# Steps 2 to 15 of a fused attention and two-layer kernel, written as one list of operations

## The chip, the cores and the metric

One core of a Trainium2 chip. The metric is the device time of one execution in microseconds. PE is TensorE, DVE is VectorE, ACT is ScalarE, POOL is GpSimd, SP is SyncE, whose queue issues the DMAs.

## The reference

Chunked attention (batch 4, 8 heads, 768 positions of 64; chunks of 32 queries see 16 positions to the left, 8 to the right and 8 memory slots), then two dense layers over 3072 tokens, 512 wide with 2048 inside:

```
for each chunk c:
    k_full = concat(mem_k, k[c*32-16 : c*32+40]);  v_full likewise
    a = softmax(q_c @ k_full.T / 8)
    out[c] = a @ v_full
x = out as 3072 x 512
x = relu(x @ moe_w_in)**2 @ moe_w_out
h = x @ moe2_w_in
return (h * tanh(softplus(h))) @ moe2_w_out
```

## The kernel before

The tokens are cut into three blocks `sb` of 1024 (four pairs `p` of 128-token tiles each, so p runs from 0 to 11), and the inner width into eight parts `j` of 256. A step is one part of one block of one layer: steps 0 to 23 are the first layer (block `s // 8`, part `s % 8`), steps 24 to 47 the second. In a step of the first layer the first weight matrix is multiplied by Strassen's scheme in the Winograd form: seven products (`product`, L587), each of six matmuls of 128x128 weights with 512 columns. Their order by name is P1, P6, P5, P2, P7, P4, P3; they accumulate in PSUM banks 0 to 2. DVE and ACT take partial sums out of the banks (`u`, L941, L948, L967) and form the four quarters of the result (L969, L975, L980), ACT applies ReLU and square (L606, L607) and rounds to a high part `g` (L600), and POOL subtracts it to give the low part (L601). The second weight matrix then takes eight units of six matmuls (`unit`, L700) in banks 3 to 5, each added by DVE to the output `y` (L714) or copied by ACT for the first part (L712). Units of step s-1 are interleaved with the products of step s. A step so has 90 matmuls of 512 columns.

Beside these run, on all engines: the attention of the next block of tokens (scores L396, maximum L414, exponentials L433, division L448 on POOL, transposes L461, their copies L482, values L506, copies L526 and sums L535 to L539 on POOL); the decoding of weights, which arrive as 64-bit numbers in halves of 512 KB (`rebias` L158 on ACT, `decode` L165 to L169 on DVE, sums L181 to L185, rounding L207 on ACT and subtraction L213 on DVE for the first layer, L225 and L232 for the second, whose parts are stored to DRAM as `w_d`); and the reading back and splitting of the blocks `x` of the next tokens (`load_x`, `split_x`, L308 on ACT and L310 on DVE). From step 8 on the first layer's weights are streamed from DRAM again, in pieces of 256 KB (`stream_w`, L259). Raw weights are loaded three halves ahead; a load is put aside by `later` and issued by the next `flush` (L141).

Steps 0 and 1 with the attention before them are a written list of single operations (the string at L1057). From step 2 (`BEGUN`) on `step` gives the order: after each product and each unit it calls `rest`, the next of 15 points of a step, which issues the weight streams and what the plans have put there with `at` (`plan_attention` at a period of 22 points, `plan_w`, `plan_sums`, and the loads and splits of x):

```
def rest():
    flush()
    i = point[0]
    if NQ <= s + 1 < STEPS and i % 2 == 0 and i < POINTS - 1:
        stream_w(s + 1, 0, i // 2)
    ...
    for w in beside.pop((s, point[0]), []):
        w()
    point[0] += 1
```

Each engine runs its instructions in the order in which they are issued here.

Of the kernel before, what the change touches and what calls it, by code (L numbers as in the profile page):

```python
# [26 lines left out]
NB = 512  # L27
# [29 lines left out]
BEGUN = 2  # L57
POINTS = 15
# [4 lines left out]
def tile_chunk_attention_moe_moe2(  # L63
# [569 lines left out]
    def block(i, s):  # L633
        ps, start, stop = {
            "1": (0, True, False), "2": (0, False, True), "6": (1, True, False), "5": (2, True, False),
            "7": (1, False, False), "4": (1, False, True), "3": (2, False, True),
        }[i]
        product(int(s), {"1": P1, "2": P2, "3": P3, "4": P4, "5": P5, "6": P6, "7": P7}[i], bank(ps), start, stop)

    def keep(i, s):  # L640
        u = u_t[i, s] = ring("u", 3, [128, NB], FP32, "u")
# [11 lines left out]
    def gated(part, s, key):  # L653
# [8 lines left out]
        elif part == "c":  # L662
            g = g_t[int(s), of[key]] = pool.tile([128, 2, NB], FP32R, tag=f"g{(4 * int(s) + i) % 7}", name="g")
            nc.scalar.copy(out=g[:, 0], in_=h_t[s, key])
        else:
            g = g_t[int(s), of[key]]
            nc.gpsimd.tensor_tensor(out=g[:, 1], in0=h_t[s, key], in1=g[:, 0].bitcast(FP32), op=ALU.subtract)

    def first_unit(i):
        w = w2_t[0].rearrange("p c (b f) -> p c b f", b=4)  # L670
        t, d = i // 4, i % 4
        order = [(f, a, 0) for f in range(2) for a in range(2)] + [(f, 0, 1) for f in range(2)]
        for n, (f, a, c) in enumerate(order):
            nc.tensor.matmul(
                out=bank(3 + i % 3),
                lhsT=w[:, a, (2 + f, f)[d // 2], d % 2 * 128:d % 2 * 128 + 128],
                rhs=g_t[0, (f, t)][:, c, :],
# [122 lines left out]
    def plan_attention(s, i, p, begun=-1):  # L800

        for n, work in {
            0: lambda: scores(p),
            1: lambda: softmax(p, 0),
            2: lambda: softmax(p, 1),
            3: lambda: (exps(p, 0), load_k(p + 1) if (p + 1) % PSB else None),
            4: lambda: exps(p, 1),
            6: lambda: normalize(p),
            8: lambda: load_v(p) if p > PSB else None,
            13: lambda: transpose_p(p),  # L810
            14: lambda: (copy_pt(p), load_q(p + 1) if (p + 1) % PSB else None),
            17: lambda: values(p),
            18: lambda: copy_x(p),
            19: lambda: sums_x(p, nc.gpsimd),
            22: lambda: store_x(p) if p != 2 * PSB - 1 else None,
        }.items():
            if n > begun:
                at(s, i + n, work)

    def plan_sums(sb):  # L820
# [32 lines left out]
        at(s, 5, lambda: later(d[:, B11], blocks()[0]))  # L853
        at(s, 9, lambda: later(d[:, B21], blocks()[1]))
        at(s, 13, first)
        at(s + 1, 0, second)
        at(s + 1, 1, fourth)
        at(s + 1, 3, third)
# [137 lines left out]
    with tc.manual_schedule():  # L996
# [18 lines left out]
        ws = [(0, i, 0) for i in range(3)], [(0, i, 1) for i in range(2)]  # L1015
        on = {"P": nc.gpsimd, "D": nc.vector}

        def rebias_first(kind, t, h):
            rebias(ws[kind][t], h, ("val", "xt2")[kind])

        def decode_first(kind, t, h):
            decode(ws[kind][t], h)
            flush()

        def split_first(kind, t, i):
            split_w(ws[kind][t], i)
            flush()
# [7 lines left out]
            "n": lambda p, h2: divide(p, h2, on["PPDDP"[p]]),  # L1035
# [4 lines left out]
            "m": lambda p, i: sums_x(p, on["PPDD"[p]], i),  # L1040
            "h": lambda p, half: place_x(p, half, 0),
            "l": lambda p, half: place_x(p, half, 1),
            "A": lambda t, h: rebias_first(0, t, h),
            "D": lambda t, h: decode_first(0, t, h),
            "S": lambda t, i: sums_w(ws[0][t], i),
            "R": lambda t, i: round_w(ws[0][t], i),
            "L": lambda t, i: split_first(0, t, i),
            "B": lambda t, h: rebias_first(1, t, h),
            "E": lambda t, h: decode_first(1, t, h),
            "F": lambda t: round_w(ws[1][t], 0),  # L1050
            "G": lambda t: split_first(1, t, 0),
            "U": first_unit,
# [172 lines left out]
```

## Time and profile before

| | us |
|---|---|
| median of 3 runs | 1077.4 |
| lowest and highest run | 1075.22 and 1477.51 |
| profiled execution | 1073.03 |
| its span, first to last instruction | 1071.2 |
| PE busy in it | 1033.5 |
| DVE busy | 853.0 |
| ACT busy | 593.3 |
| POOL busy | 426.0 |

The durations below come from the profiled execution. Ends of matmuls are modelled, so consecutive matmuls overlap in the records, and the distance of their starts is what one costs. A wait is put down to the instruction that ended last before it. In windows and groups, idle time before an instruction is that of its own engine.

### The profile page before, as it was taken

To read this page: it belongs to the slowest core of one execution; us is meant where nothing else is said; L and a number is where in the kernel's file an instruction comes from. 1 tells how busy PE (TensorE), PEld (TensorE's weight loads), DVE (VectorE), ACT (ScalarE), POOL (GpSimd) and SP (SyncE) were. 2 spreads that over 40 slices of the span, in tenths; PEclk is the share of its full clock that TensorE was granted. 3 is DMA by queue.
4 is the path that set the end of the run, shared out by engine and by line. 5 is a ranking of instruction groups with operands and counts; after the bars stand their busy time and mean duration, and the time that the engine had idled before them with its cause. 6 is when DMAs were issued, how large, how long until landed. Compare 5 with 4: busy or idle time off the path is not lost.

```text
span 1071.2 us, 19637 instructions
## 1 busy us (share of the span) xinstructions
PE 1033.5 (96%) x7288; PEld 840.2 (78%) x7295; DVE 853.0 (80%) x1154; ACT 593.3 (55%) x1160; POOL 426.0 (40%) x329
## 2 busy tenths in 40 slices
PE   6699999999999999999999999999999999999998
PEld 4577777877778888788888888888888888788887
DVE  5997899979576776789997768888858887767777
ACT  3787576766666655666565554444364443443332
POOL 1423344342334342322232255454464545545443
PEclk9999999999999999999999999999999999999999
DMA  9756876898999989899999898899989989987452
GB/s 343 286 190 252 307 278 258 292 341 284 374 359 316 340 284 327 258 373 362 349 355 333 297 319 280 293 313 353 371 291 314 327 302 369 356 255 230 147 175 79
DMA packets 191102, 319.52 MB, mean 298 GB/s; under 512 B 13472, under 2 KB 150176, under 8 KB 187168
## 3 DMA queue, kind: packets, MB, share of 16 engines
q1 hardware_dynamic: 191008, 318.27, 85.4%
q8 instruction: 58, 0.95, 0.3%
q14 instruction: 36, 0.29, 0.1%
HBM read 227.12 MB, written 91.10 MB: 297 GB/s over the span
## 4 chain that ended last, share of the span: by engine, by line
PE 59%; DVE 14%; DMA 14%; ACT 7%; issue 4%; SPq 2%; POOL 0%; DVEq 0%; ACTq 0%; POOLq 0%
PE banks L587 27%; PE banks L735 18%; PE banks L700 11%; DMA w2s<-w_d 3%; DMA w1s<-w_d 2%; DMA x<-xs_d 2%; DVE val L169 2%; DMA w_d<-val 2%; DVE y L714 2%; DVE val L168 2%; DVE val L165 1%; ACT r L607 1%; ACT p L433 1%; ACT r L606 1%; DMA q<-q_dram 1%
## 5 line engine op out<-in xcount | busy, mean ns | idle before, releaser
L587 PE MATMUL banks<-x,w1s 128*128 128x512 f32 x2016 | 493.4, 391 | 5.6 <-DVE u L967 2.2
L587 PEld LDWEIGHTS banks<-x,w1s 128*128 128x128 f32 x2016 | 376.1, 188 | 89.4 <-DVE u L967 3.7
L601 POOL TENSOR_TENSOR g<-r,g 128x512 fp32r<-128x512 f32 x182 | 253.7, 1402 | 434.7 <-ACT g L600 308.1
L700 PE MATMUL banks<-g,w2s 128*128 128x512 f32 x1104 | 266.8, 392 | 3.7 <-DVE y L714 2.2
L700 PEld LDWEIGHTS banks<-g,w2s 128*128 128x128 f32 x1104 | 205.4, 188 | 51.2 <-DVE y L714 6.1
L723 DVE TENSOR_TENSOR m<-banks,m 128x1024 f32<-128x1024 f32 (+1 forms) x145 | 175.4, 1213 | 51.8 <-PE banks L735 46.6
L735 PE MATMUL banks<-g,w2s 128*128 128x512 f32 x828 | 206.4, 389 | 0.0
L735 PEld LDWEIGHTS banks<-g,w2s 128*128 128x128 f32 x828 | 155.4, 188 | 32.4
L600 ACT CAST g<-r 128x512 fp32r<-128x512 f32 x182 | 110.7, 620 | 27.5 <-DVE r L628 23.3
L714 DVE TENSOR_TENSOR y<-banks,y 128x512 f32<-128x512 f32 x168 | 111.1, 679 | 15.3 <-PE banks L700 15.2
L601 POOL TENSOR_TENSOR g<-more,g 128x512 fp32r<-128x512 f32 x47 | 66.8, 1426 | 64.1 <-ACT g L600 37.2
L606 ACT ACTIVATE r<-r 128x512 f32<-128x512 f32 x66 | 41.7, 632 | 54.6 <-DVE r L975 38.4
L610 ACT ACTIVATE r<-r 128x512 f32<-128x512 f32 x48 | 30.3, 632 | 72.8 <-DVE r L975 37.3
L607 ACT ACTIVATE r<-r 128x512 f32<-128x512 f32 x88 | 55.7, 633 | 2.8
L232 DVE TENSOR_TENSOR val<-val,hi 128x1024 f32<-128x1024 f32 (+1 forms) x32 | 36.9, 1152 | 24.1 <-ACT hi L225 23.8
L158 ACT ACTIVATE val<-raw 128x512 f32<-128x512 f32 x64 | 40.5, 667 | 28.0 <-DMA w_d<-val 8.4
L169 DVE SCALAR_TENSOR_TENSOR val<-raw,val 128x512 uint32<-128x512 uint32 x64 | 51.7, 808 | 2.2
L225 ACT CAST hi<-val 128x1024 fp32r<-128x1024 f32 (+1 forms) x32 | 30.5, 952 | 39.6 <-DVE val L169 19.3
L165 DVE TENSOR_SCALAR val<-val 128x512 f32<-128x512 f32 x64 | 35.3, 551 | 19.7 <-ACT val L158 18.1
L941 ACT COPY u<-banks 128x512 f32<-128x512 f32 x46 | 27.1, 590 | 42.4 <-PE banks L587 42.4
L433 ACT ACTIVATE p<-banks,mneg 128x64 f32<-128x64 f32 x144 | 42.9, 335 | 2.3 <-DVE mneg L421 2.3
L967 DVE TENSOR_TENSOR u<-banks,u 128x512 f32<-128x512 f32 x46 | 31.6, 687 | 12.9 <-PE banks L587 10.2
(108 smaller groups left out, 1081.3 us busy)
## 6 DMA issues: line engine op xcount, KB each, us to landing
w1s<-w_d SPq DMA_DIRECT2D x280, 256.0 KB, 6.0
w2s<-w_d SPq DMA_DIRECT2D x229, 256.0 KB, 5.9
raw<-w_dram SPq DMA_DIRECT2D x64, 512.0 KB, 5.4
w_d<-w1s SPq DMA_DIRECT2D x8, 1792.0 KB, 7.0
x<-xs_d SPq DMA_DIRECT2D x14, 1024.0 KB, 11.4
v<-v_dram SPq DMA_DIRECT2D x24, 512.0 KB, 9.1
k<-k_dram SPq DMA_DIRECT2D x24, 368.0 KB, 6.7
w_d<-hi SPq DMA_DIRECT2D x17, 512.0 KB, 5.6
```

Source lines behind the costliest of these rows:

```text
L165: nc.vector.tensor_scalar(out=val, in0=val, scalar1=LIMIT, scalar2=-LIMIT * NEGATIVE, op0=ALU.min, op1=ALU.max)
L169: nc.vector.scalar_tensor_tensor(out=vb, in0=low, scalar=29, in1=vb, op0=ALU.logical_shift_right, op1=ALU.bitwise_or)
L433: nc.scalar.activation(out=pr[:, i], in_=s8[:, i], func=ACTF.Exp, scale=scale, bias=m[:, i:i + 1], accum_out=r_t[p][:, h2, i:i + 1],)
L587: nc.tensor.matmul(out=ps, lhsT=w[:, a, f:f + 128], rhs=x[:, xi, c, kk, :], start=start and i == 0, stop=stop and i == len(order) - 1, ski ...
L600: nc.scalar.copy(out=g[:, 0], in_=r)
L601: nc.gpsimd.tensor_tensor(out=g[:, 1], in0=r, in1=g[:, 0].bitcast(FP32), op=ALU.subtract)
L606: nc.scalar.activation(out=r, in_=h, func=ACTF.Relu)
L607: nc.scalar.activation(out=r, in_=r, func=ACTF.Square)
L700: nc.tensor.matmul(out=ps, lhsT=w[:, a, blk(f), d % 2 * 128:d % 2 * 128 + 128], rhs=g_t[s, (f, t)][:, c, :], start=i == 0, stop=i == len(o ...
L714: nc.vector.tensor_tensor(out=y, in0=ps, in1=y, op=ALU.add)
L723: engine.tensor_tensor(out=to, in0=in0, in1=in1, op=ALU.add)
L735: nc.tensor.matmul(out=bank(first + d), lhsT=w[:, a, 128 * d:128 * d + 128], rhs=g[:, c, :], start=i == 0 and blk not in ONTO, stop=i == 2 ...
```

## The change

`BEGUN` goes; `LISTED` is 16. The list, which ended with step 1, now also holds every operation of steps 2 to 15: products (P, product and step in base 36), partial sums (k), result quarters (r), the four parts of the gate (ga ReLU, gb square, gc rounding, gd POOL's subtraction), units (U, unit and step) and their evacuation (y); attention (s scores, x maximum, e exponentials, i and n division, t transposes, c copies, v values, o copies, m sums, O store; Q, K, V loads); decoding of the first layer's weights (A, D, S, R, L and B, E, F, G) and of the second's (a, d, z, w, j); loads and the two halves of splits of x (X, H, J); the six sums of the first block's output (Y); weight streams (q, with step, matrix and piece); and the issue of DMAs put aside (a dot). The products and units of a step stand in another sequence than `step` gives, and the operations of a step are mixed singly with those of its neighbours. The plans for these steps go, with `plan_attention`; from step 16 on `step` runs as before, with the ring counters set to where the list leaves off, and one split (the last of the block of step 16) left to its first point. The tokens of the part for steps 0 and 1 keep their order; the flushes that some of them did themselves are written as dots.

```diff
-BEGUN = 2
+LISTED = 2 * NQ
...
-    def first_unit(i):
+    def listed_unit(i, s):
+        w = w2_t[s].rearrange("p c (b f) -> p c b f", b=4)
...
+                out=bank(3 + (8 * s + i) % 3),
...
-    def first_y(i):
+    def listed_y(i, s):
+        _, sb, j = where(s)
         t, d = i // 4, i % 4
-        if (0, t) not in y_t:
-            y_t[0, t] = pool.tile([128, KD, NB], FP32, tag=f"y{t}", name="y")
-        nc.scalar.copy(out=y_t[0, t][:, d], in_=bank(3 + i % 3))
+        if (sb, t) not in y_t:
+            y_t[sb, t] = y_t[sb - 1, t] if sb else pool.tile([128, KD, NB], FP32, tag=f"y{t}", name="y")
+        y, ps = y_t[sb, t][:, d], bank(3 + (8 * s + i) % 3)
+        if j == 0:
+            nc.scalar.copy(out=y, in_=ps)
+        else:
+            nc.vector.tensor_tensor(out=y, in0=ps, in1=y, op=ALU.add)
...
-    def plan_attention(s, i, p, begun=-1):
...
+        sums = [
+            lambda: later(d[:, B11], blocks()[0]),
+            lambda: later(d[:, B21], blocks()[1]),
+            first,
+            second,
+            fourth,
+            third,
+        ]
+        if s < LISTED:
+            return sums
+        for work, i in zip(sums, (5, 9, 13, POINTS, POINTS + 1, POINTS + 3)):
+            at(s, i, work)
...
+            "O": store_x,
...
+            "B": lambda t, h: rebias(ws[1][t], h, "xt2" if t < NQ - 1 else "val"),
...
+            "a": lambda n, h: rebias(seconds[n], h, "val"),
+            "d": lambda n, h: decode(seconds[n], h),
+            "z": lambda n, i: sums_w(seconds[n], i),
+            "w": lambda n, i: round_w2(seconds[n], i, "xt2"),
+            "j": lambda n, i: split_w2(seconds[n], i),
+            "X": load_x,
+            "H": lambda sb, o: split_x(sb, o, 0),
+            "J": lambda sb, o: split_x(sb, o, 1),
+            "Y": lambda n: sums_y[n](),
+            "q": stream_w,
+            ".": flush,
+            "U": listed_unit,
+            "y": listed_y,
...
+            "gd110 U60 y60 G1 . r121 n40 ga101 U70 y50 gb101 gc101 gd101 y70 . P62 P12 U11 y11 U01 k12 A30 A31 "
+            "t41 t40 y01 c41 P22 . c40 k22 B20 . . D30 D31 ga200 S30 S31 K5 Q5 E20 R30 v4 L30 o40 P72 P52 . U31 "
+            "o41 gb200 gc200 k32 r222 R31 s5 x51 B21 . P42 gd200 U21 U41 x50 y31 ga211 e510 . . . P13 E21 e500 "
...
+            "U56 ga710 J13 . . P18 . k18 r127 P58 J11 q901 . J15 . gb710 . . q905 q903 y16 H14 J14 U66 q906 a00 . "
+            "Q8 P28 K8 a01 ga800 gb800 d01 . gc710 . . P68 q902 ga701 U46 H16 gc711 k28 P19 y46 d00 gb701 U76 "
...
+            "gcd11 ob1 y6c gdd11 . . P2e . a60 . ob0 r12d k2e P7e a61 d60 d61 mb0 mb1 . . k3e P5e gae00 r22e U1d "
+            "z60 z61 gad01 gbd01 gcd01 gdd01 P4e U0d w60 Ob j60 y1d gae11 gbe11 gce11 P3e . qe13 gbe00 gce00 "
+            "gde00 qg00 r21e gae10 gbe10 gce10 w61 y7c P1f U4d r12e qg03 X23 gde10 . y4d . y0d U2d y2d X20 X21 . "
...
+            ". U7d U3d j61 k1f . . P2f y3d y7d . . gae01 P6f k2f X24 gbe01 gce01 H23 J23 U5d gaf00 P7f gbf00 y5d "
+            "qg01 U6d qg05 k3f gde01 P5f P4f H20 J20 y6d U1e gde11 . H21 r22f gcf00 . P3f H24 U0e J21 . . . qg06 "
+            "r21f X25 U2e gaf11 gdf00 y1e U4e gbf11 J24 gcf11 H25 qg04 r12f y0e U3e y2e . gaf10 gbf10 gdf11 X22 "
+            "U5e H22 . J22 y4e X26 U7e y3e qg02 . . qf10 gcf10 gdf10 qf13 . gaf01 J25 gbf01 y5e gcf01 . . gdf01 "
+            "U6e H26 y7e y6e qf11 qf12"
...
-        for s in range(BEGUN, NQ):
-            if s + 1 < NQ:
-                plan_w(s, 0, (0, s + 1, 0), "Aa|D|d|RS|s|rL||||l", round_w, split_w, "val")
-                plan_w(s, 4, (0, s, 1), "A||a|D|d||R||L", round_w, split_w, "xt2")
-            else:
-                plan_w(s, 0, (0, s, 1), "A|a|D|d|R||L", round_w, split_w, "val")
-
-        seconds = [e for e in order_w if e[0]]
+                work[kind](*(int(i, 36) for i in rest))
+
         for n, e in enumerate(seconds):
-            if n < NQ - 1:
-                plan_w(NQ + n, 3, e, "Aa|D|d|RS|s|L|||||r|l", lambda e, i: round_w2(e, i, "xt2"), split_w2, "val")
-            else:
+            if n >= NQ - 1:
                 n -= NQ - 1
                 hi = (["xt0", "xt1"], ["xt2", "at1"])[n % 2]
                 plan_w(
@@ -1099,20 +1138,7 @@
                     lambda e, i, hi=hi: round_w2(e, i, hi[i]), split_w2, ("val", "at0")[n % 2],
                 )
 
-        for sb in range(NSB - 1):
-            p = PSB * (sb + 1)
-            start, first, period = ((0, 15, 22), (NQ, 10, 22))[sb]
-            if sb:
-                at(start, 0, lambda p=p: load_q(p))
-                at(start, 1, lambda p=p: load_k(p))
-            else:
-                at(BEGUN, 0, lambda p=p: load_k(p + 1))
-            for n in range(PSB):
-                if sb or n:
-                    plan_attention(start, first + period * n, p + n)
-                else:
-                    plan_attention(start, first + 2, p, 12)
-        for sb in range(NSB):
+        for sb in range(1, NSB):
             plan_sums(sb)
 
         for sb in range(1, 2 * NSB):
@@ -1125,17 +1151,15 @@
                     at(s + 3 - NQ, i + 8, lambda sb=sb, o=o: split_apart(sb, o, 0))
                     at(s + 3 - NQ, i + 9, lambda sb=sb, o=o: split_apart(sb, o, 1))
                 continue
-            if sb == 1:
-                loads, splits = (-19, -18, -9, -5, 1, 2, 4), (3, 4, 7, 8, 11, 13, 15)
-            else:
-                loads, splits = range(7), (4, 6, 8, 9, 11, 13, 14)
-            for o, i in enumerate(splits):
-                n = loads[o]
-                at(s + n // POINTS, n % POINTS, lambda sb=sb, o=o: load_x(sb, o))
-                at(s, i, lambda sb=sb, o=o: split_x(sb, o, 0))
-                at(s, i + 1, lambda sb=sb, o=o: split_x(sb, o, 1))
-        rings["g"] = rings["r"] = units[0] = 4 * BEGUN
-        for s in range(BEGUN, STEPS + 1):
+            for o, i in enumerate((4, 6, 8, 9, 11, 13, 14)):
+                if s >= LISTED:
+                    at(s, o, lambda sb=sb, o=o: load_x(sb, o))
+                    at(s, i, lambda sb=sb, o=o: split_x(sb, o, 0))
+                if s >= LISTED or (s, i + 1) == (LISTED - 1, POINTS):
+                    at(s, i + 1, lambda sb=sb, o=o: split_x(sb, o, 1))
+        rings["g"] = rings["r"] = 4 * LISTED
+        units[0] = 8 * (LISTED - 1)
+        for s in range(LISTED, STEPS + 1):
             step(s)
 
 
```

## Rows read from the trace of the kernel before

**Rows 1.** The page: span, granted clock, one transfer (issues, KB, us to landing).
```profile
span 1071.2 us, 19637 instructions
...
PEclk9999999999999999999999999999999999999999
...
w1s<-w_d SPq DMA_DIRECT2D x280, 256.0 KB, 6.0
```

**Rows 2.** Chain that ended last, in order: start, us, what.
```profile
392.29 2.00 PE banks L506 x128
...
493.90 4.08 PE banks L587 x18
```

**Rows 3.** Groups by line and shape, 93.8 to 430 us.
```profile
L700 PE MATMUL banks<-g,w2s 128*128 128x512 f32 x672 | 163.9, 393 | 2.3 <-DVE y L714 1.2 <-ACT y L712 0.8
L587 PE MATMUL banks<-x,w1s 128*128 128x512 f32 x582 | 142.5, 394 | 3.0 <-DVE u L967 2.2 <-DVE u L948 0.8
...
L168 DVE TENSOR_SCALAR val<-val 128x512 uint32<-128x512 uint32 x36 | 21.4, 594 | 1.2
...
L182 DVE TENSOR_TENSOR val<-val 128x256 f32<-128x256 f32 x12 | 8.6, 715 | 0.4
```

**Rows 4.** Timeline of PE, 290 to 308 us: start, us, group.
```profile
294.50 1.48 PE L396 MATMUL banks<-k,q 64*32 64x64 f32 x128
295.91 3.00 PE L700 MATMUL banks<-g,w2s 128*128 128x512 f32 x12
298.75 2.88 PE L587 MATMUL banks<-x,w1s 128*128 128x512 f32 x12
...
306.88 1.43 PE L587 MATMUL banks<-x,w1s 128*128 128x512 f32 x5 [1.18 <-DVE u L967]
```

**Rows 5.** Windows: length, busy PE, PEld, DVE, ACT, POOL; clock, DMA share, GB/s.
```profile
61.00:90.20 29.20, 28.64 (x123) 22.23 (x121) 27.51 (x41) 25.09 (x65) 9.90 (x7) 1.00 0.60 213
93.80:239.40 145.60, 141.08 (x1462) 114.23 (x1461) 130.50 (x203) 98.04 (x232) 54.03 (x45) 1.00 0.80 292
239.40:430.00 190.60, 186.04 (x1783) 150.67 (x1782) 136.91 (x217) 120.20 (x293) 66.91 (x56) 1.00 0.94 324
452.30:595.70 143.40, 143.02 (x631) 118.16 (x630) 128.11 (x198) 87.37 (x135) 38.44 (x27) 1.00 1.00 352
```

**Rows 6.** Waits of PE, 93.8 to 430 us: total, times, longest; six rows.
```profile
PE banks L506 <- ACT pt L482: 3.2, 6, 1.6
PE banks L587 <- DVE u L967: 2.2, 3, 1.2
PE banks L700 <- DVE y L714: 1.2, 2, 0.6
...
PE banks L384 <- ACT stage L526: 0.6, 2, 0.3
```

**Rows 7.** Timeline of three engines, 277 to 280 us.
```profile
277.38 1.30 POOL L601 TENSOR_TENSOR g<-r,g 128x512 fp32r<-128x512 f32 x1 [3.73 <-issue]
277.44 1.51 DVE L182 TENSOR_TENSOR val<-val 128x256 f32<-128x256 f32 x1
...
279.61 0.74 PE L587 MATMUL banks<-x,w1s 128*128 128x512 f32 x2 [0.67 <-DVE u L967]
```

**Rows 8.** Two lines of DVE over the whole span: least, median, longest.
```profile
L168 DVE TENSOR_SCALAR val<-val x64: 426/427/1510, 18.6 to 567.0; 128x512 uint32<-128x512 uint32 x64
...
L182 DVE TENSOR_TENSOR val<-val x24: 424/425/1509, 28.3 to 569.9; 128x256 f32<-128x256 f32 x24
```

**Rows 9.** Timeline of PE, 428 to 437 us.
```profile
435.31 1.92 PE L700 MATMUL banks<-g,w2s 128*128 128x512 f32 x6 [1.03 <-DVE y L714]
```

**Rows 10.** Waits of ACT, 93.8 to 430 us.
```profile
ACT val L158 <- DMA w_d<-val: 8.4, 3, 3.6
...
ACT val L158 <- DMA w1s<-w_d: 4.4, 1, 4.4
...
ACT val L158 <- DMA w2s<-w_d: 3.4, 1, 3.4
```

More of the change, by code (lines that the diff above doesn't have):

```diff
@@ L637, in block @@
         }[i]
-        product(int(s), {"1": P1, "2": P2, "3": P3, "4": P4, "5": P5, "6": P6, "7": P7}[i], bank(ps), start, stop)
+        product(s, {"1": P1, "2": P2, "3": P3, "4": P4, "5": P5, "6": P6, "7": P7}[i], bank(ps), start, stop)
     def keep(i, s):
-        u = u_t[i, s] = ring("u", 3, [128, NB], FP32, "u")
+        u = u_t[i, s] = pool.tile([128, NB], FP32, tag=f"u{int(i) - 1}", name="u")
         if i == "1":
@@ L674, in first_unit @@
             nc.tensor.matmul(
-                out=bank(3 + i % 3),
+                out=bank(3 + (8 * s + i) % 3),
                 lhsT=w[:, a, (2 + f, f)[d // 2], d % 2 * 128:d % 2 * 128 + 128],
-                rhs=g_t[0, (f, t)][:, c, :],
+                rhs=g_t[s, (f, t)][:, c, :],
                 start=n == 0,
@@ L798, in at @@
         beside.setdefault((s + i // POINTS, i % POINTS), []).extend(work)
-    def plan_attention(s, i, p, begun=-1):
[L802 to L818, printed above, removed]
     def plan_sums(sb):
@@ L852, in plan_sums @@
         s = (sb + 1) * NQ
[L853 to L858, printed above, removed]
+        sums = [
[10 more added lines that the diff above has]
+            at(s, i, work)
     def plan_w(s, i, e, order, round_, split, val):
@@ L1013, in tile_chunk_attention_moe_moe2 @@
             load_first[name[0]](int(name[1]))
-        ws = [(0, i, 0) for i in range(3)], [(0, i, 1) for i in range(2)]
+        ws = [[(0, i, kind) for i in range(NQ)] for kind in range(2)]
+        seconds = [e for e in order_w if e[0]]
         on = {"P": nc.gpsimd, "D": nc.vector}
[L1018 to L1027, printed above, removed]
+        sums_y = plan_sums(0)
         work = {
@@ L1034, in tile_chunk_attention_moe_moe2 @@
             "i": invert,
-            "n": lambda p, h2: divide(p, h2, on["PPDDP"[p]]),
+            "n": lambda p, h2: divide(p, h2, on["PPDDPPPPPPPP"[p]]),
             "t": transpose_p,
@@ L1072, in tile_chunk_attention_moe_moe2 @@
             elif kind == "P":
-                block(*rest)
+                block(rest[0], int(rest[1], 36))
             elif kind == "k":
-                keep(*rest)
+                keep(rest[0], int(rest[1], 36))
             elif kind == "r":
-                result(rest[:2], rest[2])
+                result(rest[:2], int(rest[2], 36))
             elif kind == "g":
-                gated(rest[0], rest[1], rest[2:])
+                gated(rest[0], int(rest[1], 36), rest[2:])
             else:
-                work[kind](*(int(i) for i in rest))
-        for s in range(BEGUN, NQ):
-            if s + 1 < NQ:
-                plan_w(s, 0, (0, s + 1, 0), "Aa|D|d|RS|s|rL||||l", round_w, split_w, "val")
-                plan_w(s, 4, (0, s, 1), "A||a|D|d||R||L", round_w, split_w, "xt2")
-            else:
-                plan_w(s, 0, (0, s, 1), "A|a|D|d|R||L", round_w, split_w, "val")
-        seconds = [e for e in order_w if e[0]]
+                work[kind](*(int(i, 36) for i in rest))
         for n, e in enumerate(seconds):
-            if n < NQ - 1:
-                plan_w(NQ + n, 3, e, "Aa|D|d|RS|s|L|||||r|l", lambda e, i: round_w2(e, i, "xt2"), split_w2, "val")
-            else:
+            if n >= NQ - 1:
                 n -= NQ - 1
```

20 lines of the change are left out of this document (8 added, 12 removed), and 64 rows, old and new, of the table work.

## The prediction, written before the change was run

> **What bounds the kernel now.** I read the page first, then the chain of waits in order of time, the groups by line and shape in the changed stretch, the windows, the waits of TensorE, and a timeline around two stalls. TensorE is busy 1033.5 us by the table above, of the 1071.2 of the page [rows 1], which shows its granted clock at nine tenths or more in every slice, so nothing here is for the clock to give: the time is TensorE's instruction count at a fixed pitch, plus whatever it waits. The pitch stands in the chain of waits: 18 matmuls of 512 columns in 4.08 us [rows 2], 0.2267 us each, and one burst of attention values (128 small matmuls) in 2.00.
>
> The stretch that the list takes over runs from 93.8 us (the second product of step 2) to 430.0 (the first product of step 16): 336.2 us. It holds 672 matmuls of the second product and 582 of the first [rows 3], 1254 x 0.2267 = 284.3 us, and the attention's bursts for the eight pairs of tiles 4 to 11: 8 of values at 2.00, 7 of scores at 1.41 (294.50 to 295.91 [rows 4]) and 7 of transposes, which I put at 0.8 (eight matmuls, an estimate between the two rates): 16.0 + 9.9 + 5.6 = 31.5. The eighth scores and transposes lie ahead of 93.8. Floor 315.8, so TensorE loses 20.4 us there. The windows [rows 5] split that: 93.8 to 239.4 (steps 2 to 7) takes 145.6 against a floor of 534 x 0.2267 + 14.6 = 135.7, so 9.9 lost; 239.4 to 430.0 (steps 8 to 15) takes 190.6 against 720 x 0.2267 + 16.8 = 180.0, so 10.6 lost. Outside, the same layer without attention, 452.3 to 595.7, takes 143.4 for seven steps of 90 x 0.2267 = 20.4, and loses 0.6. What the change can win is inside these 20.4 us, 1.9% of the span.
>
> Not all of it is a wait. After a burst the next twelve matmuls take 2.84 instead of 12 x 0.2267 = 2.72 (295.91 to 298.75 [rows 4]): 0.12 for each of 22 bursts, 2.6 us, which any order pays. The view of waits (six rows, of which four stand in [rows 6]) gives 8.8 us of open idleness in sum, every microsecond of it for DVE or ACT to empty a bank or write an operand: none for a DMA. The other 9 us are in the short gaps and the refill of TensorE's pipeline around these waits. So 8.8 is the least, 17.8 the most, that a perfect order recovers.
>
> **Why the stalls arise.** Both DVE and ACT run in program order, and the points at which the plan drops a decode of weights put three to seven operations in a lump ahead of the evacuation that TensorE needs. At 306.88 TensorE had sat 1.18 us for L967 [rows 4]. At 279.61 [rows 7] the lump is seen: DVE is at the sums behind a decode, its L182 takes 1.51 us, and only then comes L967, for which TensorE sat 0.67.
>
> That L182 is an instance of a second thing. Its least and median times are 0.424 and 0.425 us, its longest 1.509 [rows 8]; in the timeline it started 0.06 us after a POOL subtraction of 1.30 us and ended just behind it [rows 7]. L168, the decode's shift, is alike: median 0.427, longest 1.510, mean in this stretch 0.594 [rows 3, 8]. These two lines alone lose 36 x 0.167 + 12 x 0.290 = 9.5 us of DVE to it, in whole collisions of about 1 us, some ten of them. The Trainium skill has this rule ("SBUF — State Buffer", Who interferes with whom): DVE operations with two inputs in SBUF, or in a two-port mode, share a port pair with GpSimd, and whoever starts second waits for the whole instruction of the first. By that rule, which the trace agrees with, an order found from durations taken one by one can't place these collisions; it moves them. By the rule alone the time would be the second rival's, 1077; by the rows that I weigh below it is 1067.
>
> **The change part by part.** (1) Nothing is added or removed on TensorE: the same 14 x 90 matmuls of 512 columns and the same bursts, in another sequence; the new names (listed_unit, listed_y, the tags u0 to u2) issue the instructions of unit, its evacuation and the ring of three. Cost 0. (2) DVE, ACT and POOL get the same operations at other places, mixed singly with each other. What that is worth I read from each half's fill of DVE.
>
> Steps 2 to 7: at a lossless 137 us DVE's 130.5 us of work would fill 95%. The nearest rows pull apart. The one listed stretch in the trace, 61.0 to 90.2, has DVE at 27.51 of 29.20, 94%, and TensorE lost 29.2 - 120 x 0.2267 = 2.0 us, 7% (of its 123 matmuls three are the end of a burst); the hand-planned steps 17 to 23 have DVE at 128.1 of 143.4, 89%, and lose 0.6 [rows 5]. By the first row the list loses 0.07 x 145 = 10 and gains nothing; by the second it gains all but the burst cost, 9.9 - 1.2 = 8.7. I take the middle, a gain of 4, nearer to the listed row since that is the same kind of code at the same fill. Below zero: up to -4, if the seven per cent become ten.
>
> Steps 8 to 15: DVE is at 136.9 of 190.6, 72% [rows 5], so there is room on it and the waits are faults of order: between 0 and 10.6 - 1.4 = 9.2 to gain. I take 6, above the middle, because each of these waits has a free neighbour on the engine that was late.
>
> DMA: SP's queue issues the same transfers in another sequence: streams of weights for steps 8 to 16, x blocks, loads of attention, raw weights, stores. Steps 8 to 15 move 324 GB/s at a DMA share of 0.94; shortened by 9 us they would need 340, and steps 17 to 23 show 352 carried with TensorE all but unstopped [rows 5]. So I cost the moves at 0, covered by the streams' lead of a full step; if that cover goes, a transfer's landing of 6.0 us [rows 1] is the price of each one that is late. On SP's queue a load of raw weights still stands behind the decode that frees its buffer, as today; what is queued behind it there are the streams of the next step, with the step's 20.4 us as their slack.
>
> Seam: step 16 is planned by points again. Its first wait today is 1.03 us idle at 435.31 for an evacuation that stood behind a split of x [rows 9]. In the list the last split (J of block 6) still comes at that place, while the last two loads of step 15's second weights (qf11, qf12) are the very end. They meet their first use after three products (18 x 0.2267 = 4.1 us) against a landing of 6: between +2 and -1, taken as 0, since SP has only the last x loads ahead of them and can issue them early.
>
> Sum: -4 - 6 + 0 = -10 us. The profiled execution took 1073.03 us, so 1063 by its own time. The median of the runs is 1077.4, 4.4 above the profiled one (lowest 1075.2; one run of 1477 I leave aside); the same offset gives 1067.4.
>
> **Rivals.** *Everything is recovered:* the list runs like steps 17 to 23, gain 8.8 to 17.8, say 15: 1062. For it: no wait of TensorE is on a DMA and the engine totals fit. Against: DVE at 95% and the 7% lost by the listed stretch.
>
> *The collisions come back:* the list moves them. At least ten one-microsecond delays are left, and with evacuations and decode interleaved one by one a delay has an evacuation behind it more often than in the lumps. If ten of them cost TensorE about what the two cases above cost, 0.7 to 1.2 us, 10 us return and the gain is gone: 1077, give or take 4.
>
> *Slower, ACT stuck on raw weights:* ACT's first decode operation L158 today sits behind a DMA in five places in this stretch, 8.4 + 4.4 + 3.4 = 16.2 us, 3.2 each [rows 10]. The loads are issued three halves ahead and land late while the DMA engines are full, in steps 8 to 14, where the list places 14 such halves (a00 to a61) with copies and ReLUs of the products next behind them in ACT's queue. Each late one holds ACT 3.2 us; the one or two TensorE blocks (6 x 0.2267 = 1.36 each) listed next to it cover about 1.8, so 1.4 reaches TensorE: 14 x 1.4 = 20 us against 10 recovered, +10: 1087. It decides from the point where more than seven of the halves are that late. Against: today TensorE does not wait through this at all, though ACT does.
>
> *The list does not do what it says* (its order is the old one in effect): the order of products differs visibly (P6 ahead of P1, units before P5), so I give this nothing of its own; it would be 1077 too.
>
> **How the numbers follow.** Forecast (gain of 5 to 13): 0.52, 1064 to 1072. All recovered: 0.12, 1058 to 1064. Collisions come back: 0.22, 1073 to 1081. Slower: 0.14, 1082 to 1100. The likeliest is the forecast, 1067. For eight in ten I keep most of the first, the forecast, the neutral case and the nearer part of the slow one: 1060 to 1085. A change of 2% is 21.5 us, about what a measurement of this kernel tells from none. Faster by that needs more than the 20.4 us that are lost: 0.02. Slower by it is the far end of the slow case: 0.05. Within: 0.93.
>
> **What would show it.** Right: in the profile after, step 16 begins near 420; TensorE's waits from step 2 on shrink from 8.8 us to 3 or 4, and steps 8 to 15 lose less than steps 2 to 7; L168 and L182 keep means above their medians. Collisions: TensorE's waits name L967, L948 or L714 again, each behind a stretched DVE operation. Slower: ACT's idleness before L158 for DMAs grows beyond 16.2 us and TensorE waits for ACT. Wrong altogether: TensorE waits on w1s or w2s loads, which I cost at nothing.

## The result, and the profile after

| | before | changed |
|---|---|---|
| median of 6 runs, us | 1074.75 | 1058.63 |
| range without the run of 1477, us | 1069.57 to 1077.40 | 1056.84 to 1060.73 |
| span of the first profiled execution, us | 1071.2 | 1057.2 |

The ratio is 0.986 (95% interval 0.983 to 0.989): 15 us, or 1.4%, faster. The prediction said 1067, between 1060 and 1085: the direction is right, the size too small, and the time lies 1.4 us below the range.

The page of the changed kernel answers [rows 1]. Its second slice of the granted clock now shows an 8, and the landing of a weight stream is the same within 0.1 us.

```profile
span 1057.2 us, 19599 instructions
...
PEclk9899999999999999999999999999999999999999
...
w1s<-w_d SPq DMA_DIRECT2D x280, 256.0 KB, 5.9
```

In the changed kernel L587 is still the product, L674 the unit, L691 its evacuation, L645 a partial sum (before: L948, L967) and L667 POOL's subtraction. Its windows, cut at the first matmul of steps 2, 8, 16 and 17 (length, busy PE, PEld, DVE, ACT, POOL, clock, DMA share, GB/s):

```profile
89.92:231.13 141.21, 138.24 (x1455) 113.65 (x1454) 129.92 (x199) 98.95 (x239) 55.25 (x47) 0.99 0.85 304
231.13:419.46 188.33, 187.07 (x1802) 154.68 (x1800) 144.43 (x227) 124.29 (x301) 73.70 (x59) 1.00 0.99 345
419.46:439.86 20.40, 20.40 (x92) 16.90 (x90) 11.13 (x15) 8.66 (x15) 4.39 (x4) 1.00 0.57 181
```

The kernel before, cut at the same places:

```profile
90.24:239.35 149.11, 143.39 (x1473) 115.97 (x1472) 130.50 (x203) 101.51 (x239) 56.89 (x48) 1.00 0.80 295
239.35:430.03 190.68, 186.12 (x1783) 150.71 (x1782) 136.94 (x217) 120.25 (x293) 66.91 (x56) 1.00 0.94 324
430.03:452.31 22.28, 21.21 (x91) 16.66 (x90) 15.73 (x20) 14.71 (x23) 6.59 (x6) 1.00 0.83 262
```

The lengths can't be compared directly: the list finishes fewer units and bursts ahead of step 8 (1455 matmuls against 1473) and more behind it. So below, "lost" is a length less the floor of the matmuls that stand in it: 0.2267 us each of 512 columns, 2.00 a burst of values, 1.41 of scores, 0.79 of transposes, as the prediction has it. Steps 2 to 7 lost 11.3 before and 7.5 after; steps 8 to 15 lost 10.7 and 4.2; step 16 took 22.28 and 20.40, its floor. With 0.3 us ahead of step 2 and 1.6 behind step 16, that is 3.8 + 6.5 + 1.9 + 1.9 = 14.1, the 14.0 between the spans. The 1.6 is for the most part two late reads of x in steps 32 and 40 of that one profile of before (1.4 us of waits; TensorE's part behind step 16 took 618.9 there, 616.0 to 618.0 in all others, listed or not) and no effect of the change.

TensorE's waits in the list, three rows (us in total, times, longest), where [rows 6] had six and 8.8 us:

```profile
PE banks L587 <- DVE u L645: 2.2, 1, 2.2
PE banks L396 <- issue: 1.3, 1, 1.3
PE banks L674 <- DVE y L691: 0.7, 2, 0.4
```

The largest is seen in the timeline of POOL, DVE and PE (start, us):

```profile
117.67 2.71 POOL L667 TENSOR_TENSOR g<-r,g 128x512 fp32r<-128x512 f32 x2 [1.43 <-ACT g L664]
117.77 1.48 DVE L165 TENSOR_SCALAR val<-val 128x512 f32<-128x512 f32 x1
...
119.28 1.39 DVE L168 TENSOR_SCALAR val<-val 128x512 uint32<-128x512 uint32 x1
...
121.31 0.68 DVE L645 TENSOR_TENSOR u<-banks,u 128x512 f32<-128x512 f32 x1
122.05 2.93 PE L587 MATMUL banks<-x,w1s 128*128 128x512 f32 x6 [2.17 <-DVE u L645]
```

Two subtractions follow each other on POOL, and each of the two decode operations beside them (0.43 us alone, [rows 8]) takes some 1.4: 2 us, and the sum that frees the bank stands behind them. What comes next is the clock: 3.4 us at half, 1.2 GHz, where 8 matmuls start instead of 15, directly after that idleness.

```profile
122.00:125.40 3.40, 3.35 (x8) 2.68 (x9) 2.87 (x5) 1.95 (x5) 0.00 (x0) 0.50 0.73 261
```

The groups of the listed stretch beside [rows 3]: L168 has kept its mean (590 ns, 594 before), L182 has not (507, 715 before).

```profile
L168 DVE TENSOR_SCALAR val<-val 128x512 uint32<-128x512 uint32 x36 | 21.2, 590 | 1.2
...
L182 DVE TENSOR_TENSOR val<-val 128x256 f32<-128x256 f32 x12 | 6.1, 507 | 0.4
```

Over all lines of DVE in this stretch I counted the operations that took at least 0.25 us more than the shortest of their line and shape: 46 before, with 28.7 us more in sum, and 44 after, with 31.2.

### The profile page after: what moved, and what is told of

It is laid out like the page before. It is cut to its first block, busy times and chain, and to the rows that moved or that the text cites. A ratio compares the mean times of both kernels' runs of the same rounds, so it can differ in the third digit from the quotient of the medians.

```text
span 1057.2 us, 19599 instructions
## 1 busy us (share of the span) xinstructions
PE 1030.7 (97%) x7288; PEld 842.3 (80%) x7295; DVE 854.9 (81%) x1154; ACT 589.0 (56%) x1160; POOL 428.4 (41%) x329
## 4 chain that ended last, share of the span: by engine, by line
PE 87%; DVE 9%; issue 2%; DMA 1%; ACT 1%; SPq 0%; DVEq 0%
PE banks L587 40%; PE banks L740 21%; PE banks L674 13%; PE banks L705 8%; PE banks L396 1%; DVE val L168 1%; DVE val L169 1%; DVE val L165 1%; PE banks L506 1%; PE banks L783 1%; PE banks L461 1%; DVE y L691 1%; DMA k<-k_dram 1%; DVE x L553 1%; DMA q<-q_dram 1%
## 5 line engine op out<-in xcount | busy, mean ns | idle before, releaser
L587 PE MATMUL banks<-x,w1s 128*128 128x512 f32 x2016 | 495.4, 391 | 3.0 <-DVE u L645 2.2
L587 PEld LDWEIGHTS banks<-x,w1s 128*128 128x128 f32 x2016 | 377.9, 188 | 84.4 <-DVE u L645 3.3
L601 POOL TENSOR_TENSOR g<-r,g 128x512 fp32r<-128x512 f32 x126 | 177.6, 1420 | 252.5 <-ACT g L600 140.6
L740 PE MATMUL banks<-g,w2s 128*128 128x512 f32 x828 | 206.5, 389 | 0.0
L740 PEld LDWEIGHTS banks<-g,w2s 128*128 128x128 f32 x828 | 155.4, 188 | 32.4
L674 PE MATMUL banks<-g,w2s 128*128 128x512 f32 x720 | 178.1, 393 | 1.3 <-DVE y L691 0.7
L667 POOL TENSOR_TENSOR g<-r,g 128x512 fp32r<-128x512 f32 x64 | 94.2, 1482 | 186.4 <-ACT g L664 161.4
L674 PEld LDWEIGHTS banks<-g,w2s 128*128 128x128 f32 x720 | 134.1, 188 | 30.7 <-ACT y L689 1.8
L705 PE MATMUL banks<-g,w2s 128*128 128x512 f32 x432 | 102.6, 389 | 0.5 <-ACT u L932 0.5
L705 PEld LDWEIGHTS banks<-g,w2s 128*128 128x128 f32 x432 | 81.0, 188 | 17.6 <-ACT u L932 0.9
L600 ACT CAST g<-r 128x512 fp32r<-128x512 f32 x126 | 76.1, 621 | 25.7 <-DVE r L628 23.3
L691 DVE TENSOR_TENSOR y<-banks,y 128x512 f32<-128x512 f32 x104 | 69.1, 682 | 23.3 <-PE banks L674 22.8
L610 ACT ACTIVATE r<-r 128x512 f32<-128x512 f32 x48 | 30.4, 633 | 72.2 <-DVE r L966 37.3
L169 DVE SCALAR_TENSOR_TENSOR val<-raw,val 128x512 uint32<-128x512 uint32 x64 | 48.5, 758 | 2.2
L932 ACT COPY u<-banks 128x512 f32<-128x512 f32 x32 | 18.8, 586 | 43.5 <-PE banks L587 43.5
L664 ACT CAST g<-r 128x512 fp32r<-128x512 f32 x64 | 39.6, 623 | 5.3 <-PE banks L674 4.4
```

The lines of the kernel that those rows point to most:

```text
L169: nc.vector.scalar_tensor_tensor(out=vb, in0=low, scalar=29, in1=vb, op0=ALU.logical_shift_right, op1=ALU.bitwise_or)
L587: nc.tensor.matmul(out=ps, lhsT=w[:, a, f:f + 128], rhs=x[:, xi, c, kk, :], start=start and i == 0, stop=stop and i == len(order) - 1, ski ...
L600: nc.scalar.copy(out=g[:, 0], in_=r)
L601: nc.gpsimd.tensor_tensor(out=g[:, 1], in0=r, in1=g[:, 0].bitcast(FP32), op=ALU.subtract)
L674: nc.tensor.matmul(out=bank(3 + (8 * s + i) % 3), lhsT=w[:, a, (2 + f, f)[d // 2], d % 2 * 128:d % 2 * 128 + 128], rhs=g_t[s, (f, t)][:, c ...
L691: nc.vector.tensor_tensor(out=y, in0=ps, in1=y, op=ALU.add)
```

## The experiments

**Again, and each half alone.** First the changed kernel once more, then a kernel with the list up to step 7 and the plans from step 8, and one the other way round.

> The changed kernel once more, as the base of the three runs beside it. My theory (the order of evacuations on DVE and ACT): the ratio to the kernel before stays at 0.983 to 0.989, and the one large wait of the first profile (2.17 us for a partial sum of step 3, behind two DVE operations that each met a POOL subtraction, then 3.4 us at half the granted clock) comes again, since the order on each engine is fixed. Rival (chance of the run): the wait is gone or elsewhere, and the time scatters by some 4 us between runs. The 1.6 us that were won behind step 17, where nothing was changed: if they belong to the list's other order of DMAs, steps 32 and 40 again begin without the waits for x of the kernel before (0.7 and 1.2 us lost there); if they were chance, some of that is back.

1059.92 us, ratio 0.985 (0.983 to 0.988). The second profile has the first one's losses (7.6, 5.2, and 20.40 for step 16) with the same wait of 2.2 us, now at 123.

```diff
-LISTED = 2 * NQ
+LISTED = NQ
...
+        at(NQ, 0, lambda: load_q(2 * PSB))
+        at(NQ, 1, lambda: load_k(2 * PSB))
+        for n in range(PSB):
+            plan_attention(NQ, 10 + 22 * n, 2 * PSB + n)
+        for sb in range(NSB):
```

> The list for steps 2 to 7 alone, points from step 8 on. My theory: steps 2 to 7 lose about 7.5 us as in the changed kernel (11.3 before), steps 8 to 15 about 10.7 and step 16 about 1.9 as before, so -4 us, ratio 0.996. Rival (the halves hang together, since the list draws work of step 8 forward and leaves products of step 7 behind): a seam at step 8 eats the 4 us or more, ratio 1.00 or above.

1074.64 us, ratio 0.999 (0.997 to 1.001). The stretch to step 8 lost 13.1 us, but 5.6 of it in the last 11 us, where the list meets the points (timeline of PE):

```profile
234.98 2.93 PE L674 MATMUL banks<-g,w2s 128*128 128x512 f32 x6 [2.93 <-DVE y L691]
238.69 1.66 PE L674 MATMUL banks<-g,w2s 128*128 128x512 f32 x6 [0.78 <-DVE y L691]
```

Up to there it lost 7.5, as in the whole list. Steps 8 to 15 by points lost 12.6.

```diff
+BEGUN = 2
...
+        )
+        for s in range(BEGUN, NQ):
+            if s + 1 < NQ:
+                plan_w(s, 0, (0, s + 1, 0), "Aa|D|d|RS|s|rL||||l", round_w, split_w, "val")
...
+        for s in range(BEGUN, NQ):
+            step(s)
```

> Points for steps 2 to 7, the list for steps 8 to 15 alone. My theory: steps 2 to 7 lose 11.3 as before, steps 8 to 15 about 4.2 (10.7 before), step 16 nothing (1.9 before): -8.4 us, ratio 0.992, and the sum of this run and the run with steps 2 to 7 is the whole change. If the gain behind step 17 belongs to the DMAs of the list's second half, -10 and 0.9905. Rival (the halves hang together): less than 5 us.

1077.6 us, ratio 1.002 (1.001 to 1.004): 0.2% slower. At the seam 14.1 us went (timeline of PE, one line further down in the code):

```profile
249.29 4.60 PE L588 MATMUL banks<-x,w1s 128*128 128x512 f32 x12 [3.65 <-ACT u L644]
257.37 2.90 PE L588 MATMUL banks<-x,w1s 128*128 128x512 f32 x6 [3.49 <-DMA w1s<-w_d]
262.58 0.85 PE L397 MATMUL banks<-k,q 64*32 64x64 f32 x64 [2.31 <-DMA k<-k_dram]
```

The list starts the products of step 9 soon after those of step 8 and counts on streams and loads that it issues itself ahead of step 8. From 266 us to step 16 it lost 4.9; from 266 us on, the points lost 8.8 (first profile of before) and 12.5 (the kernel with steps 2 to 7 alone). Step 16 took 20.40 here, 22.21 there. So my theory, that each half brings its share by itself, fell as a statement on the two kernels. It holds inside each half; in how far the seams are the list's property or only come from where I cut, these two don't tell.

**One sum ahead of the decode.** Run beside the last three:

```diff
-            "D40 k23 gb210 gb201 F2 n50 n51 t51 O4 gc210 y51 P23 G2 gb211 gc211 P73 . U61 . S40 R40 gd210 U22 . . "
+            "k23 D40 gb210 gb201 F2 n50 n51 t51 O4 gc210 y51 P23 G2 gb211 gc211 P73 . U61 . S40 R40 gd210 U22 . . "
```

> The changed kernel with one exchange: the partial sum of step 3 (k23) ahead of the decode of a half (D40) instead of behind it on DVE. My theory (an evacuation behind a lump that meets POOL): the 2.17 us wait goes, with it the stretch at half clock that cost 1.4 us more, so -3.5 us against the changed kernel, ratio to the kernel before 0.9825. Rival (DVE is full in steps 2 to 7, so a delay taken out at one place comes back at the next evacuation): 0 to -1 us.

1057.85 us, ratio 0.984 (0.981 to 0.986), 2 us under the changed kernel beside it, which the intervals don't separate. The profile does: steps 2 to 7 lost 5.5 instead of 7.6, the stretch of half clock is gone, and the next collision shows as a wait of 1.2 us. So the sum of step 3 brought some 2 us, between what my theory and the rival expected.

**The kernel before, profiled again.**

> The kernel before once more, for a second profile. In 23 runs its median is 1075.6, the first profiled execution took 1073.0. My theory (the prediction's sum was made against an execution of the fast end): the second profile is longer than 1071.2 in span, by new waits inside steps 2 to 16, above 20.4 + 1.9 us lost there; the time behind step 17 is 616 to 617.5, not 618.9. Rival (the offset lies outside the span, in the launch): the same span and the same losses.

1079.0 us, span 1076.3, 5.1 above the first profile of the same kernel. Steps 2 to 7 lost 12.5 (11.3 in the first), steps 8 to 15 lost 16.2 (10.7), step 16 took 22.22 and the rest 617.5. The windows of steps 2 to 7 and 8 to 15:

```profile
90.11:240.42 150.31, 144.94 (x1473) 117.41 (x1472) 130.36 (x203) 101.75 (x239) 56.18 (x48) 0.99 0.79 293
240.42:436.61 196.19, 188.54 (x1783) 151.57 (x1782) 136.20 (x217) 121.13 (x293) 66.05 (x56) 0.99 0.92 317
```

What came on top is in the timeline of PE and two windows; the last row is the first profile of before at the place of the window of 136.70 us:

```profile
296.50 1.07 PE L396 MATMUL banks<-k,q 64*32 64x64 f32 x85
300.81 0.92 PE L396 MATMUL banks<-k,q 64*32 64x64 f32 x43 [3.24 <-issue]
...
136.70:140.10 3.40, 3.40 (x93) 3.14 (x86) 3.33 (x6) 1.20 (x3) 1.50 (x1) 0.50 0.46 158
300.60:304.00 3.40, 3.19 (x49) 2.53 (x49) 0.86 (x2) 2.43 (x11) 0.00 (x0) 0.50 0.90 326
...
135.60:139.00 3.40, 3.21 (x132) 2.93 (x133) 3.30 (x6) 2.18 (x4) 1.37 (x2) 1.00 0.25 72
```

In the middle of a burst of scores (pair 9) TensorE stops for 3.24 us and waits for nothing that the profile shows; then its clock is at half. Neither is in the first profile. At 135.5 us it waits 1.58 us for L482 and then runs at half; in the first profile it waits 1.59 there and keeps its clock.

**Without the collisions.** Of the 46 stretched operations of DVE, 29 ran beside POOL's subtractions, which read two tiles; a fill with zeros reads none. Both kernels were run with that fill in the first layer; they leave out the low part of the gate's result there.

```diff
-        nc.gpsimd.tensor_tensor(out=g[:, 1], in0=r, in1=g[:, 0].bitcast(FP32), op=ALU.subtract)
+        if where(s)[0] == 0:
+            nc.gpsimd.memset(g[:, 1].bitcast(FP32), 0.0)
+        else:
+            nc.gpsimd.tensor_tensor(out=g[:, 1], in0=r, in1=g[:, 0].bitcast(FP32), op=ALU.subtract)
...
-            nc.gpsimd.tensor_tensor(out=g[:, 1], in0=h_t[s, key], in1=g[:, 0].bitcast(FP32), op=ALU.subtract)
+            nc.gpsimd.memset(g[:, 1].bitcast(FP32), 0.0)
```

> The kernel before, with POOL's subtraction for the low part of the gate (L601) in the first layer put out for a fill with zeros, which reads nothing; this leaves the low part out of the first layer. It takes away most of DVE's collisions with POOL. Theory lumps (the place of a decode ahead of an evacuation makes the waits of the kernel before): steps 2 to 15 still lose 14 us or more of 21.9, ratio 0.993 or above. Rival, collisions (the stretched operations make them): they lose 10 or less, ratio 0.988 or below. In both the means of L165, L168 and L169 come down to their medians.

> The changed kernel with the same fill with zeros in place of POOL's subtraction in the first layer (its low part is left out). The one large wait of the changed kernel was behind two collisions, so it goes with the half clock behind it: both theories expect -4 us against the changed kernel, ratio to the kernel before 0.981 to 0.983. If lumps made the waits of the kernel before, the list is then ahead of the kernel before with the same fill by 12 us or more; if collisions made them, by 5 or less.

Before with the fill: 1067.13 us, ratio 0.992 (0.990 to 0.995). Steps 2 to 7 lost 5.8 instead of 12 (11.9 by the means of the two profiles of before), steps 8 to 15 still 13.2:

```profile
89.64:233.28 143.64, 141.40 (x1473) 116.30 (x1472) 120.95 (x203) 101.77 (x239) 31.37 (x46) 1.00 0.84 306
233.28:426.48 193.20, 188.06 (x1783) 152.11 (x1782) 132.37 (x217) 121.18 (x293) 39.85 (x56) 0.99 0.92 322
```

With the list: 1054.57, ratio 0.980 (0.977 to 0.983), 2.6 and 5.6 lost. So the fill takes away about half of what the points lose in steps 2 to 7, and the list keeps a lead of 12.5 us beside it. The half is not all collisions: the fill takes POOL 0.53 us where the subtraction takes 1.36, and with it went a wait of TensorE for POOL's division, 1.20 us in both profiles of before (the first one's row):

```profile
92.96 1.09 PE L461 MATMUL banks<-cst,p 128*128 128x128 f32 x8 [1.20 <-POOL p L448]
```

In steps 8 to 15 little went: the 13.2 hold a pause of 2.4 us in the scores of pair 9, and 1.6 us for the half clock behind it, and the first profile of before lost 10.7 without either. Some collisions remain, beside POOL's other operations and in a few cases beside the fill: 20 stretched operations in the first kernel. The means of L165 and L168 (608 and 493 ns) did not come down to their medians (420 and 427), as both theories had expected.

**A fuller DVE.** The decode's clamp a second time on 36 tiles of the changed kernel, which changes no value: 22 x 0.42 = 9.2 us more of DVE in steps 2 to 7, 14 x 0.42 = 5.9 in steps 8 to 15.

```diff
+        if 5 <= order_w.index(e) <= 22:
+            nc.vector.tensor_scalar(
+                out=val, in0=val, scalar1=LIMIT, scalar2=-LIMIT * NEGATIVE, op0=ALU.min, op1=ALU.max
+            )
```

> The changed kernel with the clamp of each decoded half of the list's steps (L165) issued twice, which changes no value: 36 more DVE operations of 0.42 us, 22 of them in steps 2 to 7 (9.2 us) and 14 in steps 8 to 15 (5.9 us). Theory fill (the prediction's: in steps 2 to 7 DVE is as good as full): steps 2 to 7 grow by 6 to 9 us, steps 8 to 15 by at most 1; ratio 0.992. Rival, slack (DVE's idle time is spread so that each evacuation has some): under 3 us in all, ratio 0.988 or below.

1071.12 us, ratio 0.996 (0.994 to 0.997). Windows and TensorE's waits (lines moved by four):

```profile
89.90:241.18 151.28, 141.16 (x1456) 114.47 (x1455) 139.01 (x220) 98.92 (x239) 55.29 (x47) 0.98 0.79 284
241.18:432.21 191.03, 187.50 (x1802) 154.47 (x1800) 150.94 (x242) 123.69 (x301) 71.89 (x59) 1.00 0.97 340
...
PE banks L591 <- DVE u L649: 7.7, 5, 2.6
PE banks L678 <- DVE y L695: 4.1, 4, 2.0
PE banks L400 <- issue: 1.9, 1, 1.9
```

In steps 2 to 7, where DVE is 92% full, 9.2 us of work cost 10.1, of which 1.6 is a second stretch of half clock; in steps 8 to 15, at 77%, 5.9 cost 2.7 (6.9 lost instead of 4.2), or 1.7 against its second profile. Both are above the 6 to 9 and the at most 1 that the theory gave; the rival's 3 in all is far off.

**Three moves in the list.** The sum of the fourth kernel, the same for k24, and the scores of pair 9 in two halves with a product between them:

```diff
-    def scores(p):
+    def scores(p, *tiles):
...
-            "D40 k23 gb210
+            "k23 D40 gb210
-            S50 B40 x61 m50 x60 k24 m51
+            k24 S50 B40 x61 m50 x60 m51
-            o81 s9 x90 . . gd911 qa05 gb910 qa10 qb05 P7a gc910
+            o81 s90 . . gd911 qa05 gb910 qa10 qb05 P7a s91 x90 gc910
```

> The list with three exchanges: the partial sum of step 3 (k23) ahead of a decode as in the run before, the same for the partial sum of step 4 (k24, ahead of the sums S50 and the maximum x61), and the scores of pair 9 issued in two halves with one product (P7 of step 10) between. In every profile of this study but the first one of the kernel before, TensorE sits inside that burst, at the same place of its instruction stream, for 1.3 to 3.4 us and waits for nothing that the profile shows. Theory (evacuation behind a lump; and a stream of instructions that runs dry in a burst of 256 in 1.5 us): the 1.2 us wait at k24 and the 1.5 us in the scores both go, -2.5 us against the run with k23 alone, ratio 0.981. Rivals: k24's wait moves to the next evacuation (-1.5 us only); the pause in the scores is not the burst's, and comes with the same length in the second half (-1 us only).

1055.29 us, ratio 0.981 (0.979 to 0.984): the fastest kernel that leaves nothing out. Steps 2 to 15 lost 4.1 + 2.9 (5.5 + 4.2 with the sum of step 3 alone), of which 2.6 is the price of the bursts that the prediction counts, and the only waits left are these, 1.1 us:

```profile
PE banks L674 <- DVE y L691: 0.7, 2, 0.4
PE banks L674 <- DVE w2s L213: 0.4, 1, 0.4
```

**The pause and the seam, in the kernel before.** The same halving of the scores by its plan, and the DVE half of the third block's splits one point later:

```diff
-            0: lambda: scores(p),
-            1: lambda: softmax(p, 0),
+            0: lambda: scores(p, 0) if p == 9 else scores(p),
+            1: lambda: (scores(p, 1) if p == 9 else None, softmax(p, 0)),
```

> The kernel before with the scores of pair 9 issued in two halves, one point (six matmuls, 1.36 us) apart. Theory: the pause in that burst (3.2 us in the second profile of the kernel before, 0 in the first) and the 3.4 us at half clock behind it are what most runs of the kernel before have beyond its first profile; spread over 2.9 us the burst meets it less: ratio 0.996 to 0.998, and no idleness at L396 that waits for nothing. Rival (the pause comes with a full DMA load, whatever TensorE does): ratio 1.00, the pause in the second half or behind it.

1074.39 us, ratio 0.999 (0.998 to 1.001): no change, as the rival had it. In its profile the pause took 1.45 us and no half clock followed, but steps 8 to 15 lost 12.9. The two profiles of before had pauses of 0 and 3.24, so one profile does not show that the halving shortened it:

```profile
295.88 0.86 PE L396 MATMUL banks<-k,q 64*32 64x64 f32 x64
296.66 1.81 PE L700 MATMUL banks<-g,w2s 128*128 128x512 f32 x6
298.40 0.34 PE L396 MATMUL banks<-k,q 64*32 64x64 f32 x15
300.19 0.73 PE L396 MATMUL banks<-k,q 64*32 64x64 f32 x49 [1.45 <-issue]
```

It falls after 64 + 6 + 15 = 85 matmuls, as in the undivided burst of the second profile: its place goes by TensorE's instruction, not by the burst.

```diff
-                at(s, i + 1, lambda sb=sb, o=o: split_x(sb, o, 1))
+                at(s, i + 1 + (sb == 2), lambda sb=sb, o=o: split_x(sb, o, 1))
```

> The kernel before with DVE's half of each split of x for the third block one point later, so that the evacuation of step 16's first unit is not behind it. Theory (the 1.9 us lost in step 16 before the change are that order and nothing of the list): step 16 takes 20.4 to 20.9 us instead of 22.2, the rest stays. Rival: the split's other half on ACT, behind the gate of step 15, is what was late; then DVE waits there as before and step 16 keeps 21.5 or more.

1074.19 us in one run. Step 16 took 21.67 instead of 22.22, and TensorE's wait there went over to ACT:

```profile
438.83 2.55 PE L700 MATMUL banks<-g,w2s 128*128 128x512 f32 x10 [0.98 <-ACT u L941]
```

So the splits of x held both engines there, not DVE alone, and moving one half only hands the wait on, as the rival had it.

## Why the prediction was right in kind and short in size

*The signs.* Those named for "right" came: step 16 begins at 419.5, TensorE's waits from step 2 on are 4.2 us, steps 8 to 15 lose less than steps 2 to 7, and L168 and L182 keep means above their medians. What failed are two terms of the sum, the offset and the seam.

*Steps 2 to 7, "a gain of 4": right.* 3.8 in the first profiles, 4.4 by the means of two each (11.9 to 7.5). The 4 was taken from the middle of 0 to 8.7, between two rows that pulled apart, so that it is met this closely is luck. The reason stands too: at this fill of DVE an added microsecond of DVE costs a microsecond of TensorE (the clamp), and the list still loses there until two sums are put ahead of the work in front of them. One sentence was inexact: the list has lumps as well (D30 D31); what it changes is which side of the lump an evacuation stands on.

*Steps 8 to 15, "I take 6": right against the profile that it was read from* (6.5), too small against the runs. The waits were for the most part faults of order, as said: with the fill the points still lose 13.2 there, 9.2 of it without the pause and the half clock.

*The seam, "taken as 0": wrong.* Step 16 won 1.9 us, in every kernel whose list reaches it (20.40) and in none that enters it by points (21.67 to 22.32). I priced only the last two weight loads and left [rows 9] as it was. But step 16 also gets what earlier steps leave over. By groups of the step, three DVE halves of splits of x (L310, 4.2 us) fell into it before, with three ACT halves (L308, 3.0 us); after, one and none:

```profile
L310 DVE TENSOR_TENSOR x<-xt,x 128x1024 fp32r<-128x1024 f32 x1 | 1.2, 1218 | 0.0
```

In all DVE has 11.13 us of work there instead of 15.73 and ACT 8.66 instead of 14.71, and the wait of [rows 9] is gone. The list had got the others done ahead of step 16.

*"The same offset gives 1067.4": the step that failed most.* I took the 4.4 us between the profiled execution and the median for something that any kernel carries along. In the changed kernel it is -0.3: its profiled execution took 1058.96 us, its median is 1058.63. Of the 8.8 us between 1067.4 and this median, 4.7 are the offset, 1.9 the seam, 1.9 what the first profile of before lost ahead of step 2 and behind step 16, and 0.3 the steps 2 to 15.

The offset was too large from the start. The 1077.4 is the middle of three runs, and one of the three is the 1477 that I said I leave aside; 23 later runs of the same kernel have a median of 1075.6, 2.6 above the profiled execution. And that rest is not carried along either. The second profile shows where such microseconds sit: 1.2 and 5.5 of the 6.7 that it loses more are in steps 2 to 15, in the pause of pair 9 and two stretches of half clock, inside what the list replaces. The first profile of before is at the fast end: three others of kernels with the points (second profile, split scores, seam) lost 12.5 to 12.7 and 12.9 to 16.2. By means of two profiles the change is -4.4 - 8.7 - 1.9 = -15.0 us, which is the 15 of the runs; against the first profile alone, my -10 would have been -12 with the seam right. In the list the pause took 1.3 and 1.6 us in its two profiles, without half clock behind it.

*The rivals.* "Everything is recovered" has its time, 1058 to 1064, close by, but not its mechanism: 11.7 us are still lost, 4.7 of which the three moves take back. "The collisions come back" fell as a cost: they are as many as before (44 for 46), and TensorE's one wait for DVE of more than a microsecond is behind two of them, 2.2 us and the half clock behind it. The Trainium skill's rule ("SBUF — State Buffer", Who interferes with whom), that whoever starts second on the shared port waits for the whole instruction of the first, agrees with the trace at 117.67, where each of two operations took 1 us longer. It tells that they collide and not who waits for it. "ACT stuck on raw weights" fell: that idleness of ACT went from 16.2 us to 1.4. Its wait for the stores of the rounded parts grew instead, from 3.8 to 12.2 us, and none of TensorE's three rows of waits names it:

```profile
ACT hi L225 <- DMA w_d<-hi: 12.2, 6, 3.7
...
ACT val L158 <- DMA w_d<-val: 1.4, 2, 0.9
```

*Transfers at 0: right.* Steps 8 to 15 moved 345 GB/s at a DMA share of 0.99, and no row of TensorE's waits in the changed kernel's first profile names a load; the second has one of 0.2 us in these steps.

*Open:* whether the sequence of products or the places of DVE's operations bring more. The two are bound by the evacuations of the banks, and no kernel with one alone was tried. And why the clock fell after 1.57 to 1.59 us of idleness ahead of one and the same burst of values, near 135 us, in four profiles with the points and not in two others.

## What to carry to other kernels

A gap between the profiled execution and the median is not a constant to add to any forecast: take a second profile, and see whether its extra microseconds lie in the stretch that the change replaces. Cost a seam by all the work that the change takes out of the step behind it, not only by what it leaves late. And when an order is found from durations taken one by one, look at the few waits that remain one by one: here three moves of single operations were worth some 4 us more.

## What the hardware showed that was not expected

TensorE pauses in the scores of pair 9 without a semaphore to wait for, 1.3 to 3.2 us (not 3.4, as I had it ahead of the three moves) in eleven of thirteen profiles, always some 6,590 instructions into its program. The burst issues 256 instructions (128 loads of weights, 128 matmuls) in 1.5 us, 10 us behind a burst of values, and instructions arrive by a DMA queue of their own, 58 packets of 16 KB (MB behind the count):

```profile
q8 instruction: 58, 0.95, 0.4%
```

The traces hold the time of each packet, and by these times TensorE waits for its instructions there. In all eleven profiles it goes on 1.2 to 1.6 us after the 25th packet has landed. In the second profile of before that packet started at 298.30 us, when TensorE had stopped already, and landed at 299.36; TensorE went on at 300.81. In the first it started at 290.00. The queue's row for 289.9 to 290.2 us of the first profile, then for 298.2 to 298.4 of the second:

```profile
q8 instruction: 1, 0.02, 22.6%
...
q8 instruction: 1, 0.02, 33.2%
```

In the two profiles without a pause (the first of before, and the three moves) the packet had landed 4.2 and 1.3 us before TensorE came to the place. The fixed place has a reason too: 58 packets for some 15,000 of TensorE's instructions are one for about 256, and the longer pauses of this kind in the attention ahead of step 2 stand at about 450, 963, 1218 and 1986 instructions, each a multiple of 256 (within 3) ahead of 6,595, where the pause stands in the profiles with the fullest record. Why the packet came 8 us later in one execution than in another of the same kernel stays open, and so does whether spreading the burst helps.

An idle stretch of TensorE can cost more than its length: after 1.58, 2.17 and 3.24 us of idleness the granted clock stood at 0.50 for the next 3.4 us. In the changed kernel 8 matmuls started there where 15 would at full clock, a further 7 x 0.2267 = 1.6 us. Not every such idleness does it: after the pause of pair 9, 1.3 and 1.6 us in its two profiles, the clock stayed at full.
